# Attention block on one core: the last unit's sums gathered, inverted as 8 columns and spread; partial projections in TensorE's waits; zero products at a higher level

## Chip, cores and metric

One core of one Trainium2 chip. The metric is the device time in microseconds (us) of one execution, the median over runs.

## The reference

Multi-head self-attention with an output projection, in bfloat16, for x of shape (1, 2048, 448), 16 heads of 28:

```python
qkv = (x @ wqkv).reshape(B, S, 3, H, Dh).transpose(2, 0, 3, 1, 4)
q, k, v = qkv[0], qkv[1], qkv[2]
p = softmax(einsum("bhqd,bhkd->bhqk", q, k) * Dh ** -0.5, axis=-1)
o = einsum("bhqk,bhkd->bhqd", p, v)
return o.transpose(0, 2, 1, 3).reshape(B, S, D) @ wo
```

## The kernel before, in words

The work is cut into 16 units: four groups `g` of four heads, and four chunks `c` of 512 queries. In a unit, for each of 16 key tiles `kt` of 128 keys, a "row" is four score tiles of 128 keys by 512 queries, one per head. A score product (L899, TensorE) goes to a PSUM bank; most rows are turned into probabilities by ScalarE's exponential (L961, groups of three and two tiles that alternate between banks 0 to 2 and 3 to 4), into a ring of 43 tile slots `PT`. The 67 rows listed in `PLAN["rows"]` go to VectorE instead, which builds an approximate exponential with integer arithmetic: `DY` (L923, one per head), then two shifted copies `DS` (L931), with three buffers each. The products with V (L866) accumulate a whole unit in one bank of the pool `M` (banks 5 to 7). V has a column of ones, so that row 28 of each head's 32 holds the sum of the softmax.

Behind its last product a unit is normalised. Units 0 to 13 do it through DRAM (L732 to L742). Unit 14 does it on TensorE (`norm_pe`): `N1` (L761) gathers the sums, 4 columns for each 128 queries, by a product of the float copy `OTS` with the selector `SEL`; one reciprocal of 16 columns; `N2` (L772) spreads the inverse over 32 rows per head by products with the identity `id_f`; and a multiply (L776) writes `OTN`. Unit 15, `last_unit` (L781), stands alone at the end. It works in two halves `k` of 256 queries: copy to `OTS` (L803), `BC` (L810), which spreads the sums with the matrix `EX`, a reciprocal of 128x256 into `RB` (L814), the multiply `NM` (L816). Its output projection is split: `OPA` (L792) is three of four groups of heads for each of four output tiles, opened as soon as the score banks (pool `T`) come free, and `OPB` (L833) adds the last group. `out_tile` copies the tile to `OUTS` (ScalarE for even tiles, L699, VectorE for odd, L701) and sends it to DRAM (L703, on ScalarE's queue or SP's). `N1` (L823) and `RS` (L828) then compute the same sums' inverses once more for a range check (L993 to L1005); every engine loads the resulting FLAG at the end (L1689) and branches on it.

The order on each engine is fixed when the program is built, by a list planner (`_Prog.schedule`): every operation has a priority (low goes first), an estimated duration and dependencies; the planner takes on each engine what can start first and, within a look-ahead, what has the lowest priority. `fill_to` puts zero products ("Z", L484, four products of 512 columns that add zero) on TensorE where a gap is long enough or where the activity planned in the last 3413 ns is below a level:

```python
must = 0.0 if -60.0 < nxt.prio < -20.0 or t < self.HOT_UNTIL else CFG["hotm"] if t < CFG["hot1"] else self.FILL_HOT if nxt.kind == "r" and nxt.act > 200.0 else self.FILL_MUST
if level >= self.FILL_TARGET or (level >= must and gap < fd + 15.0):
    return
```

`FILL_HOT` is the level ahead of a score group; `CFG` and `PLAN` hold priorities and the rows and times of the late projections.

Of the kernel before, what the change touches and what calls it, by code (L numbers as in the profile page):

```python
# [7 lines left out]
ALU = mybir.AluOpType  # L8
AX = mybir.AxisListType
FP32 = mybir.dt.float32  # L10
# [53 lines left out]
class _Prog:  # L64
# [276 lines left out]
ZLO = -ZADD  # L341


CFG = {"late": 4.5, "load": 1.5, "load0": 18, "dcost": 2.3, "dlead": 29.327663454, "aslack": 234.39592858, "opp": 0.0, "oload": 2.5, "klead": 0.397755013, "vlag": 0.106640586, "hot1": 45000.0, "hotm": 3600.0, "nslack": 2479.300775199, "dlook": 20.0, "plook": 474.412241514, "rcost": 4.9, "rlead": 1.0, "rend": 4, "rgap": 2, "acost": 0.4455, "dprio": 0.107516791, "nride": 4, "rslack": 300.0, "stail": 24, "jprio": -1.32365559, "sdlap": 1.959518579, "vwlead": 0.625380571, "sdpen": 5.516852626, "rcostx": -0.000676632}

PLAN = {
    "rows": [8, 14, 16, 23, 24, 28, 36, 40, 42, 48, 51, 52, 55, 61, 62, 72, 73, 74, 82, 86, 92, 95, 96, 100, 101, 107, 109, 110, 113, 118, 121, 127, 133, 135, 136, 140, 141, 147, 150, 151, 160, 162, 165, 172, 174, 176, 178, 182, 186, 187, 190, 191, 193, 196, 201, 208, 213, 214, 218, 219, 222, 229, 230, 232, 236, 241, 244],
    "late": [1.077995674, 1.833905636, 2.095141755, 1.212792363, 3.137574495, 1.671785065, 2.075848527, 2.120471152, 2.256950028, 2.271931426, 2.394850262, 3.571309667, 3.864949717, 3.254719197, 2.824659682, 4.377919272, 3.673227809, 4.718144519, 3.955221706, 4.65154477, 4.74737354, 7.012401197, 6.732080085, 7.708659606, 5.168205011, 6.425448937, 5.787055861, 6.854207722, 8.35329498, 10.189712555, 7.674620861, 7.367372235, 8.08547084, 7.336648721, 7.808454674, 8.789731951, 8.769658309, 8.528783968],
}


def _fast(nc, x, wqkv, wo, out, n_heads=16):
# [10 lines left out]
    QCH = 512  # L363
# [18 lines left out]
    units = [(g, c) for g in range(G) for c in range(NCH)]  # L382
# [3 lines left out]
    P = _Prog()  # L386
    es = ExitStack()
    with es:
# [5 lines left out]
        OTN = XO[:, :].rearrange("p (g s) -> p g s", s=S)  # L394
# [60 lines left out]
        def dma_of(t, g):  # L455
# [3 lines left out]
                      dur=300, prio=-12, name="iota")  # L459
# [8 lines left out]
        def zero_pass(acc_open, t):  # L468
# [12 lines left out]
            def emit(e):  # L481
                ins = None
                for h in range(4):
# [15 lines left out]
        ex_op = P.add("dve", (lambda e: e.tensor_copy(EX.rearrange("p (h r) -> p h r", r=32), SEL.rearrange("p (h o) -> p h o", o=1).to_broadcast([128, 4, 32]))),  # L499
                      deps=[sel_op], dur=250, prio=5.0, name="ex")  # L500
        grp_wo = _DmaGroup("wo")
        dma_wo = []
        for g in range(G):
# [117 lines left out]
        rows = PLAN["rows"]  # L621
        if rows is None:
# [5 lines left out]
            rows = []  # L628
# [66 lines left out]
        def out_tile(n, opm, hold, eng, pr):  # L695
            oi = outs_n[0] % NOB
            outs_n[0] += 1
            if eng == "act":
                fe = (lambda e: e.activation(OUTS[:, oi, :], bank(hold.banks[0])[:, 0:D], AF.Identity))  # L699
            else:  # L700
                fe = (lambda e: e.tensor_copy(OUTS[:, oi, :], bank(hold.banks[0])[:, 0:D]))  # L701
            opev = P.add(eng, fe, deps=[opm, outs_last[oi]], dur=550, prio=pr, name=f"OPEV{n}", rel=[(hold, 0)])
            outs_last[oi] = P.add("act" if eng == "act" else "sp", (lambda e: e.dma_start(of[n * 128:(n + 1) * 128, :], OUTS[:, oi, :])),  # L703
                                  deps=[opev], after=[outs_last[oi]], dur=60, prio=pr, name=f"ODMA{n}", dma_group=grp_out[oi],
                                  nbytes=128 * D * 2)
# [75 lines left out]
        def last_unit(u, last_pv):  # L781
            g, c = units[u]
            ub = u % 2
            pr = u - 50.0
            open_ops = []
            for j in range(NQT):
                n = c * NQT + j
                hold = []

                for gg in range(G - 1):  # L790
                    def f_part(e, n=n, hold=hold, gg=gg):
                        return e.matmul(bank(hold[0].banks[0])[:, 0:D], OTN[:, gg, n * 128:(n + 1) * 128], wop[:, gg, :],  # L792
                                        start=(gg == 0), stop=False, skip_group_check=True)
                    op = P.add("pe", f_part, deps=([otn_ev[(g_, c)] for g_ in range(G - 1)] + dma_wo[-1:]) if gg == 0 else [], after=hold[-1:], kind="f", units=0.9, act=448.0,
                               prio=-34.9, name=f"OPA{n}_{gg}", acq=("T", 1) if gg == 0 else None)
                    if gg == 0:
                        hold.append(op)
                open_ops.append((n, hold, op))
            HF = QCH // 2
            evs = []  # L800
            for k in range(2):
                sl = slice(k * HF, (k + 1) * HF)
                evs.append(P.add("dve", (lambda e, sl=sl: e.tensor_copy(OTS[:, ub, sl], bank(pv_open[u].banks[0])[:, sl])),  # L803
                                 deps=[last_pv, ots_last[ub]], after=evs[-1:], dur=340, prio=pr, name=f"ACCEV{u}_{k}", rel=[(pv_open[u], 0)] if k else []))
            bcs, n1s, rss, nms = [], [], [], []
            for k in range(2):
                sl = slice(k * HF, (k + 1) * HF)

                def f_bc(e, k=k, sl=sl):
                    return e.matmul(bank(bcs[k].banks[0])[:, sl], EX, OTS[:, ub, sl], start=True, stop=True)  # L810
                bcs.append(P.add("pe", f_bc, deps=[evs[k], ex_op], after=bcs[-1:], dur=480, prio=pr - 1.0, name=f"BC{u}_{k}", acq=("M", 1)))
            for k in range(2):
                sl = slice(k * HF, (k + 1) * HF)
                rb = P.add("dve", (lambda e, sl=sl, k=k: e.reciprocal(RB[:, ub, sl], bank(bcs[k].banks[0])[:, sl])),  # L814
                           deps=[bcs[k], ots_last[ub]], after=nms[-1:], dur=340, prio=pr - 1.0, name=f"RB{u}_{k}", rel=[(bcs[k], 0)])
                nms.append(P.add("dve", (lambda e, sl=sl: e.tensor_tensor(OTN[:, g, c * QCH + sl.start:c * QCH + sl.stop], RB[:, ub, sl], OTS[:, ub, sl], ALU.mult)),  # L816
                                 deps=[rb, evs[k]], after=nms[-1:], dur=340, prio=pr - 1.0, name=f"NM{u}_{k}"))
            for k in range(2):
                def f_n1(e, k=k):
                    b = n1s[k].banks[0]  # L820
                    ins = None
                    for qt in (2 * k, 2 * k + 1):
                        ins = e.matmul(bank(b)[:, qt * 4:(qt + 1) * 4], OTS[:, ub, qt * 128:(qt + 1) * 128], SEL[:, :], start=True, stop=True)  # L823
                    return ins
                n1s.append(P.add("pe", f_n1, deps=[evs[k], sel_op], after=n1s[-1:] + bcs[-1:], dur=430, prio=-34.85, name=f"N1_{u}_{k}", acq=("M", 1)))
            for k in range(2):
                i0 = u * 16 + 8 * k
                rss.append(P.add("dve", (lambda e, k=k, i0=i0: e.reciprocal(RS[:, i0:i0 + 8], bank(n1s[k].banks[0])[:, 8 * k:8 * k + 8])),  # L828
                                 deps=[n1s[k]], after=rss[-1:] + nms[-1:], dur=120, prio=-34.0, name=f"RS{u}_{k}", rel=[(n1s[k], 0)]))
                rs_last.append(rss[-1])  # L830
            for j, (n, hold, op) in enumerate(open_ops):
                def f_fin(e, n=n, hold=hold):
                    return e.matmul(bank(hold[0].banks[0])[:, 0:D], OTN[:, g, n * 128:(n + 1) * 128], wop[:, g, :], start=False, stop=True, skip_group_check=True)  # L833
                fin = P.add("pe", f_fin, deps=[nms[j // 2]], after=[op], kind="f", units=0.9, act=448.0, prio=pr - 1.0, name=f"OPB{n}")
# [912 lines left out]
```

## Time and profile before

| what | value |
|---|---|
| time, median of 3 runs | 366.27 us (365.79 to 367.6) |
| the profiled execution's own time | 365.65 us |
| its span, first to last instruction | 363.8 us |
| mean granted TensorE clock | 0.997 |
| PE / DVE / ACT busy | 345.0 / 327.5 / 345.7 us |
| exponentials on ScalarE | 303, from 9.77 us to about 353.9 us |

PE is TensorE (PEld its weight loads), DVE VectorE, ACT ScalarE, SP the queue that issues most transfers. In the timeline's rows the numbers are start, duration, engine, line, operation, output<-input, shapes and count; in brackets the idle time before and what ended it. Group rows end with busy time and the mean of one in ns, then the idle time before and what ended it. A row of waits has the total, the times and the longest. A row of a stretch has its length, then busy time and count of PE, PEld, DVE, ACT and POOL, the granted clock, the share of the transfers' engines and GB/s. A matmul's end is modelled, so durations of matmuls that follow each other overlap.

### The profile page before, as it was taken

The page shows a single profiled execution, that of the slowest core. Times are in us where ns is not written, and L with a number is a line of the kernel's source. Part 1 is how long each engine was busy: PE and PEld are TensorE (multiplying, and loading weights), DVE is VectorE, ACT ScalarE, POOL GpSimd, SP SyncE. Part 2 cuts the span into 40 slices and gives each one's busy share as a digit, 9 for nine tenths or more (in the row PEclk, how much of TensorE's full clock was granted, in tenths as well). Part 3 has the DMA queues.
Part 4 walks back from the last instruction along what each step waited for, and adds up shares of the span by engine and source line. Part 5 has one row for each costly group of instructions (what it writes and reads, how often), then busy time and mean ns, then how long its engine had stood idle before and what let it go on. Part 6 is the DMA issues. An engine that isn't in the chain of part 4 may idle for free.

```text
span 363.8 us, 8769 instructions
## 1 busy us (share of the span) xinstructions
PE 345.0 (95%) x3845; PEld 115.1 (32%) x3845; DVE 327.5 (90%) x577; ACT 345.7 (95%) x307; POOL 3.4 (1%) x9
## 2 busy tenths in 40 slices
PE   8999999999999999999999999999998999999995
PEld 4433322333223422233233322332222222223332
DVE  6577999989999999999999999999999999989517
ACT  1999999999999999999999999999999999999991
POOL 3000000000000000000000000000000000000000
PEclk9999999999999999999999999999999999999998
DMA  8500000000000010000100000000000000020201
GB/s 247 134 2 3 3 30 5 19 15 4 30 2 5 32 32 2 3 31 3 28 7 16 20 4 30 3 24 12 30 3 4 30 5 31 4 80 3 77 29 51
DMA packets 13939, 9.89 MB, mean 27 GB/s; under 512 B 7504, under 2 KB 12048, under 8 KB 13896
## 3 DMA queue, kind: packets, MB, share of 16 engines
q1 hardware_dynamic: 13096, 8.74, 8.1%
q8 instruction: 30, 0.49, 0.6%
q10 hardware_dynamic: 800, 0.56, 0.5%
q14 instruction: 13, 0.11, 0.1%
HBM read 7.23 MB, written 2.06 MB: 26 GB/s over the span
## 4 chain that ended last, share of the span: by engine, by line
ACT 80%; PE 17%; DVE 3%; issue 0%
ACT PT L961 80%; PE ps L899 5%; PE ps L866 4%; PE ps L558 2%; PE ps L484 2%; DVE RB L814 1%; PE ps L713 1%; PE ps L575 1%; DVE DY L923 1%; PE ps L541 1%; PE ps L792 0%; DVE DS L931 0%; PE ps L761 0%; PE ps L772 0%; DVE XO L816 0%
## 5 line engine op out<-in xcount | busy, mean ns | idle before, releaser
L961 ACT ACTIVATE PT<-ps 128x1536 bf16<-128x1536 f32 (+1 forms) x303 | 342.7, 1400 | 1.9 <-PE ps L899 1.6
L923 DVE TENSOR_SCALAR DY<-ps 128x512 int16<-128x512 f32 x268 | 175.6, 682 | 10.4 <-PE ps L899 9.2
L899 PE MATMUL ps<-QT,KT 28*128 28x512 bf16 x1024 | 153.1, 384 | 12.2 <-ACT PT L961 6.9
L931 DVE TENSOR_SCALAR DS<-DY 128x2048 int16<-128x2048 int16 x134 | 89.5, 680 | 0.7
L899 PEld LDWEIGHTS ps<-QT,KT 28*128 28x128 bf16 x1024 | 39.8, 91 | 138.5 <-ACT PT L961 101.2
L866 PE MATMUL ps<-PT,V 128*32 128x512 bf16 x756 | 66.5, 385 | 0.9 <-DVE V L531 0.5
L866 PE MATMUL ps<-DS,VW 128*32 128x512 f16 x536 | 48.2, 386 | 0.0
L558 PE MATMUL ps<-xT,w_raw 112*32 112x512 bf16 x512 | 35.8, 381 | 0.1
L484 PE MATMUL ps<-ZM,ZW 128*32 128x512 bf16 x312 | 28.8, 412 | 1.2 <-DVE ZM L466 1.2
L866 PE MATMUL ps<-DY,V 128*32 128x512 f16 x268 | 26.5, 385 | 0.2 <-DVE OTS L726 0.2
L866 PEld LDWEIGHTS ps<-PT,V 128*32 128x32 bf16 x756 | 16.6, 94 | 30.0 <-issue 23.5
L866 PEld LDWEIGHTS ps<-DS,VW 128*32 128x32 bf16 x536 | 12.1, 94 | 21.1 <-issue 16.4
L575 PE MATMUL ps<-w_raw,xT 112*128 112x112 bf16 x256 | 17.3, 214 | 0.0
L558 PEld LDWEIGHTS ps<-xT,w_raw 112*32 112x32 bf16 x512 | 12.5, 95 | 12.9 <-issue 2.9
L701 DVE CAST OUTS<-ps 128x448 bf16<-128x448 f32 x14 | 8.7, 623 | 8.4 <-PE ps L713 8.1
L575 PEld LDWEIGHTS ps<-w_raw,xT 112*128 112x128 bf16 x256 | 13.0, 98 | 6.5 <-issue 4.3
L531 DVE CAST KT<-ps 128x512 bf16<-128x512 f32 x16 | 11.0, 686 | 3.2 <-PE ps L558 3.0
L531 DVE CAST V<-ps 128x448 bf16<-128x448 f32 x16 | 9.9, 618 | 2.6 <-PE ps L575 2.6
L484 PEld LDWEIGHTS ps<-ZM,ZW 128*32 128x32 bf16 x312 | 7.6, 99 | 12.5 <-issue 10.0
L713 PE MATMUL ps<-wop,XO 128*128 128x448 bf16 x48 | 11.5, 355 | 0.0
L529 DVE TENSOR_SCALAR QT<-ps 128x512 bf16<-128x512 f32 x15 | 10.2, 683 | 0.4 <-PE ps L558 0.4
L726 DVE COPY OTS<-ps 128x512 f32<-128x512 f32 x15 | 10.2, 682 | 0.4 <-PE ps L866 0.4
(51 smaller groups left out, 83.8 us busy)
## 6 DMA issues: line engine op xcount, KB each, us to landing
RB<-scr_r SPq DMA_DIRECT2D x14, 256.0 KB
out_dram<-OUTS SPq DMA_DIRECT2D x14, 112.0 KB, 1.7
XO<-in_x_dram SPq DMA_DIRECT2D x3, 448.0 KB, 6.3
w_raw<-in_wqkv_dram SPq DMA_DIRECT2D x5, 196.0 KB, 6.0
wop<-in_wo_dram SPq DMA_DIRECT2D x16, 24.5 KB
XO<-in_x_dram SPq DMA_DIRECT2D x1, 224.0 KB, 3.1
XO<-in_x_dram ACTq DMA_DIRECT2D x1, 224.0 KB, 3.5
scr_l<-OTS SPq DMA_DIRECT2D x14, 8.0 KB
```

The lines of the kernel that those rows point to most:

```text
L484: ins = e.matmul(ps[32 * h:32 * h + 32, b * 512:(b + 1) * 512], ZW[:, :], ZM[:, :], start=shut, stop=shut, skip_group_check=not shut, tile ...
L529: fe = (lambda e: e.tensor_scalar(evac[0](), evac[1](hold[0].banks[0]), mul, None, ALU.mult))
L531: fe = (lambda e: e.tensor_copy(evac[0](), evac[1](hold[0].banks[0])))
L558: ins = e.matmul(ps[32 * h:32 * h + 32, b * 512:(b + 1) * 512], w_raw[0:IT, it, col:col + 32], xT[0:IT, it, c * 512:(c + 1) * 512], start= ...
L575: ins = e.matmul(ps[:, b * 512 + j * GD:b * 512 + (j + 1) * GD], xT[0:IT, it, n * 128:(n + 1) * 128], w_raw[0:IT, it, 2 * D + g * GD:2 * D ...
L713: return e.matmul(bank(hold[0].banks[0])[:, 0:D], OTN[:, gg, n * 128:(n + 1) * 128], wop[:, gg, :], start=(gg == 0), stop=(gg == G - 1))
L726: accev = P.add("dve", (lambda e: e.tensor_copy(OTS[:, ub, :], bank(pv_open[u].banks[0]))), deps=[last_pv, ots_last[ub]], dur=610, prio=pr ...
L866: ins = e.matmul(ps[32 * h:32 * h + 32, b * 512:(b + 1) * 512], weights(k, h), p_[h], start=(kt == 0 and k == 0), stop=(kt == NK - 1 and k ...
L899: ins = e.matmul(bank(b), KT[32 * h:32 * h + rows, g, kt * 128:(kt + 1) * 128], QT[32 * h:32 * h + rows, g, c * QCH:(c + 1) * QCH], start= ...
L923: o1 = P.add("dve", (lambda e, ri=ri, h=h, s=s: e.tensor_scalar(DY[:, ri, h * 512:(h + 1) * 512], bank(s.banks[0]), ZLO, ZADD, ALU.max, AL ...
L931: row_ev[r] = [P.add("dve", (lambda e, k=k: e.tensor_scalar(DS[:, k, rk, :], DY[:, ri, :], float(PHASE[k + 1]), None, ALU.add)), deps=row_ ...
L961: ex = P.add("act", (lambda e, p0=p0, w=w, bf=bf: e.activation(PT[:, p0 * 512:(p0 + w) * 512], bank(bf(), w), AF.Exp, scale=ESCALE)), deps ...
```

## The change

In the last unit `BC`, the two 128x256 reciprocals and `EX` are gone. `N1` and `RS` take their place on the way to `NM`; `N2` spreads the 8 inverted columns of a half over 256 columns, and `NM` reads them from PSUM. Of the twelve `OPA` products the last four are held back to stand in TensorE's order behind `N1`, `N2`, `N2` and the second `OPB`. `FILL_HOT` rises from 2787.5 to 3300. `PLAN` and some priorities in `CFG` are new: again 67 rows on VectorE, others than before, and other times for the 38 late projections.

```diff
-    FILL_HOT = 2787.5
+    FILL_HOT = 3300.0
...
-CFG = {... "dlead": 29.327663454, "aslack": 234.39592858, ... "klead": 0.397755013, "vlag": 0.106640586, ... "nslack": 2479.300775199, ... "dprio": 0.107516791, ... "jprio": -1.32365559, "sdlap": 1.959518579, "vwlead": 0.625380571, "sdpen": 5.516852626 ...}
+CFG = {... "dlead": 30.385592406, "aslack": 235.147215477, ... "klead": 0.405674492, "vlag": 0.024622608, ... "nslack": 2585.717981114, ... "dprio": 0.651412491, ... "jprio": -0.750113813, "sdlap": 4.771128299, "vwlead": 1.249363626, "sdpen": 6.528606395 ...}
...
-    "rows": [... 150, 151, 160, 162, 165, 172, 174, 176, ... 219, 222, 229, 230, 232, 236, 241, 244],
+    "rows": [... 149, 152, 162, 163, 164, 165, 169, 176, ... 215, 222, 229, 231, 234, 235, 244, 248],
...
-        EX = iota_i[:, :].bitcast(FP32)
-        ex_op = P.add("dve", ...)
...
-            bcs, n1s, rss, nms = [], [], [], []
...
-                    return e.matmul(bank(bcs[k].banks[0])[:, sl], EX, OTS[:, ub, sl], start=True, stop=True)
...
-                rb = P.add("dve", (lambda e, sl=sl, k=k: e.reciprocal(RB[:, ub, sl], bank(bcs[k].banks[0])[:, sl])),
-                           deps=[bcs[k], ots_last[ub]], after=nms[-1:], dur=340, prio=pr - 1.0, name=f"RB{u}_{k}", rel=[(bcs[k], 0)])
...
+            n1s, rss, n2s, nms = [], [], [], []
...
-                n1s.append(P.add("pe", f_n1, ..., prio=-34.85, ...))
+                n1s.append(P.add("pe", f_n1, deps=[evs[k], sel_op], after=n1s[-1:], dur=430, prio=pr, name=f"N1_{u}_{k}", acq=("M", 1)))
             for k in range(2):
                 i0 = u * 16 + 8 * k
                 rss.append(P.add("dve", (... e.reciprocal(RS[:, i0:i0 + 8], bank(n1s[k].banks[0])[:, 8 * k:8 * k + 8])),
-                                 deps=[n1s[k]], after=rss[-1:] + nms[-1:], dur=120, prio=-34.0, ...))
+                                 deps=[n1s[k]], after=rss[-1:], dur=200, prio=pr, ...))
+                def f_n2(e, k=k):
+                    for qt in (2 * k, 2 * k + 1):
+                        for h in range(4):
+                            i = u * 16 + qt * 4 + h
+                            ins = e.matmul(ps[32 * h:32 * h + 32, b * 512 + qt * 128:b * 512 + (qt + 1) * 128],
+                                           RS[:, i:i + 1].to_broadcast([128, 32]), id_f[:, :], start=True, stop=True, tile_position=(0, 32 * h))
+                n2s.append(P.add("pe", f_n2, deps=[rss[k]], after=n2s[-1:], dur=400, prio=pr, name=f"N2_{u}_{k}", acq=("M", 1)))
+                nms.append(P.add("dve", (... e.tensor_tensor(OTN[...], bank(n2s[k].banks[0])[:, sl], OTS[:, ub, sl], ALU.mult)),
+                                 deps=[n2s[k]], after=nms[-1:], dur=340, prio=pr, ...))
...
-                fin = P.add("pe", f_fin, ..., prio=pr - 1.0, name=f"OPB{n}")
+                fin = P.add("pe", f_fin, ..., prio=pr if j < 2 else -34.8, name=f"OPB{n}")
+                opb.append(fin)
...
+            for part, behind in ((8, n1s[1]), (9, n2s[1]), (10, n2s[1]), (11, opb[1])):
+                parts_[part].after.append(behind)
+                parts_[part].prio = -36.0
```

More of the change, by code (lines that the diff above doesn't have):

```diff
@@ L349 @@
+    "late": [1.281070854, 1.964014751, 1.915657661, 0.76, 2.743900482, 1.159356603, 1.904466413, 1.845975994, 2.106524837, 2.189415295, 2.428349574, 2.873971098, 2.728623137, 3.84085501, 2.733578841, 4.131340808, 3.508351422, 5.446684044, 4.832243098, 4.46548081, 5.163206443, 7.002171665, 6.90767575, 7.804407036, 4.947925744, 6.78739139, 5.302922841, 6.89552453, 9.777227448, 10.389677342, 7.735503962, 7.490566717, 8.23514301, 7.360578973, 7.83742904, 10.319692841, 8.329224918, 8.680463746],
 }
@@ L784, in last_unit @@
             pr = u - 50.0
-            open_ops = []
+            open_ops, parts_ = [], []
             for j in range(NQT):
@@ L804, in last_unit @@
                                  deps=[last_pv, ots_last[ub]], after=evs[-1:], dur=340, prio=pr, name=f"ACCEV{u}_{k}", rel=[(pv_open[u], 0)] if k else []))
-            bcs, n1s, rss, nms = [], [], [], []
[L806 to L814, printed above, removed]
-                           deps=[bcs[k], ots_last[ub]], after=nms[-1:], dur=340, prio=pr - 1.0, name=f"RB{u}_{k}", rel=[(bcs[k], 0)])
-                nms.append(P.add("dve", (lambda e, sl=sl: e.tensor_tensor(OTN[:, g, c * QCH + sl.start:c * QCH + sl.stop], RB[:, ub, sl], OTS[:, ub, sl], ALU.mult)),
-                                 deps=[rb, evs[k]], after=nms[-1:], dur=340, prio=pr - 1.0, name=f"NM{u}_{k}"))
+            n1s, rss, n2s, nms = [], [], [], []
             for k in range(2):
@@ L828, in last_unit @@
                 rss.append(P.add("dve", (lambda e, k=k, i0=i0: e.reciprocal(RS[:, i0:i0 + 8], bank(n1s[k].banks[0])[:, 8 * k:8 * k + 8])),
-                                 deps=[n1s[k]], after=rss[-1:] + nms[-1:], dur=120, prio=-34.0, name=f"RS{u}_{k}", rel=[(n1s[k], 0)]))
+                                 deps=[n1s[k]], after=rss[-1:], dur=200, prio=pr, name=f"RS{u}_{k}", rel=[(n1s[k], 0)]))
                 rs_last.append(rss[-1])
+                def f_n2(e, k=k):
+                    b = n2s[k].banks[0]
+                    ins = None
+                    for qt in (2 * k, 2 * k + 1):
[3 more added lines that the diff above has]
+                                           RS[:, i:i + 1].to_broadcast([128, 32]), id_f[:, :], start=True, stop=True, tile_position=(0, 32 * h))
+                    return ins
+                n2s.append(P.add("pe", f_n2, deps=[rss[k]], after=n2s[-1:], dur=400, prio=pr, name=f"N2_{u}_{k}", acq=("M", 1)))
+                sl = slice(k * HF, (k + 1) * HF)
+                nms.append(P.add("dve", (lambda e, sl=sl, k=k: e.tensor_tensor(OTN[:, g, c * QCH + sl.start:c * QCH + sl.stop], bank(n2s[k].banks[0])[:, sl], OTS[:, ub, sl], ALU.mult)),
+                                 deps=[n2s[k]], after=nms[-1:], dur=340, prio=pr, name=f"NM{u}_{k}", rel=[(n2s[k], 0)]))
+            opb = []
             for j, (n, hold, op) in enumerate(open_ops):
@@ L833, in f_fin @@
                     return e.matmul(bank(hold[0].banks[0])[:, 0:D], OTN[:, g, n * 128:(n + 1) * 128], wop[:, g, :], start=False, stop=True, skip_group_check=True)
-                fin = P.add("pe", f_fin, deps=[nms[j // 2]], after=[op], kind="f", units=0.9, act=448.0, prio=pr - 1.0, name=f"OPB{n}")
+                fin = P.add("pe", f_fin, deps=[nms[j // 2]], after=[op], kind="f", units=0.9, act=448.0, prio=pr if j < 2 else -34.8, name=f"OPB{n}")
+                opb.append(fin)
                 out_tile(n, fin, hold[0], "act" if j % 2 == 0 else "dve", pr)
+            for part, behind in ((8, n1s[1]), (9, n2s[1]), (10, n2s[1]), (11, opb[1])):
+                parts_[part].after.append(behind)
+                parts_[part].prio = -36.0
         def pv(u, kt):
```

9 lines of the change are left out of this document (3 added, 6 removed).

## The prediction

> **What bounds the kernel now.** I read the page's busy shares first, then the groups, the waits, the chain, and last the timeline of the final 12 us.
>
> ```profile
> PE 345.0 (95%) x3845; PEld 115.1 (32%) x3845; DVE 327.5 (90%) x577; ACT 345.7 (95%) x307; POOL 3.4 (1%) x9
> PEclk9999999999999999999999999999999999999998
> L961 ACT ACTIVATE PT<-ps 128x1536 bf16<-128x1536 f32 (+1 forms) x303 | 342.7, 1400 | 1.9 <-PE ps L899 1.6
> ```
>
> Three engines are 90% busy or more, so the shares alone decide nothing. The group row does: ScalarE's 303 exponentials take 342.7 us of the 363.8 us span and sat idle for 1.9 us before all of them together. ScalarE sets the pace from the first exponential to the last.
>
> ```profile
> PEld ps L899 <- ACT PT L961: 101.2, 271, 0.7
> ACT PT L961 <- PE ps L899: 1.6, 3, 0.6
> 334.50 2.37 ACT L961 ACTIVATE PT<-ps 128x1536 bf16<-128x1536 f32 x2 [0.51 <-PE ps L899]
> 337.45 6.88 ACT L961 ACTIVATE PT<-ps 128x1536 bf16<-128x1536 f32 x6 [0.59 <-PE ps L899]
> ```
>
> These are waits (total, times, longest). TensorE's queue stood 101.2 us, 271 times, until ScalarE gave back a score bank; ScalarE stood 1.6 us for TensorE, in three places. Two of the three lie at 334 and 337 us, 1.1 us together; the third is the start. So the exponentials can lose at most about 1.1 us more of idle time, and the place to gain is behind the last one. The chain there:
>
> ```profile
> 354.31 0.67 PE ps L792 x3
> 354.99 0.57 PE ps L810 x2
> 355.58 1.77 DVE RB L814
> 357.38 0.43 DVE XO L816
> 357.80 1.68 DVE RB L814
> 359.50 0.44 DVE XO L816
> 359.98 0.55 PE ps L833 x2
> 360.54 0.79 PE ps L823 x8
> 361.32 0.89 PE ps L484 x12
> 362.25 0.18 PE ps L1002
> 362.45 0.15 DVE FLAG L1005
> ```
>
> From about 354.3 us on nothing but the last unit's normalisation and projection runs. Two reciprocals of 128x256 elements (RB) take 3.45 us of it. Behind the last projections (359.98) come the reciprocal sums for the flag (L823), zero products (L484), the flag, and the exit.
>
> **The change part by part, first the tail.** Removed: the two spreading products BC, the two RB reciprocals, the start-up copy EX. Moved up from the flag's path onto the main path: the gather N1 (SEL times OTS) and the 8-column reciprocals RS. Added: N2, which spreads the 8 columns with 16 small float products per half, in the form that unit 14 already uses (L772). The rows for the prices:
>
> ```profile
> 354.37 0.76 DVE L803 COPY OTS<-ps 128x256 f32<-128x256 f32 x2 [3.92 <-PE ps L866]
> 354.85 0.73 PEld L810 LDWEIGHTS ps<-OTS,iota_i 128*128 128x128 f32 x4 [0.30 <-DVE OTS L803]
> 332.65 0.83 PE L761 MATMUL ps<-SEL,OTS 128*128 128x4 f32 x6
> 333.74 0.39 PE L761 MATMUL ps<-SEL,OTS 128*128 128x4 f32 x2
> 336.00 1.08 PE L772 MATMUL ps<-id_f,RS 128*32 128x128 f32 x32
> L772 PE MATMUL ps<-id_f,RS 128*32 128x128 f32 x32 | 1.1, 276 | 0.0
> 361.11 0.45 DVE L828 RECIPROCAL RS<-ps 128x8 f32<-128x8 f32 x2
> 359.85 1.35 DVE L701 CAST OUTS<-ps 128x448 bf16<-128x448 f32 x2
> 360.49 0.33 SPq L703 DMA_DIRECT2D out_dram<-OUTS  x1
> 360.49 1.07 SPq L703 DMA_DIRECT2D out_dram<-OUTS  x2
> out_dram<-OUTS SPq DMA_DIRECT2D x3, 112.0 KB, 1.7
> 362.00:362.50 0.50, 0.37 (x5) 0.08 (x1) 0.23 (x2) 0.00 (x0) 0.00 (x0) 0.50 1.04 355
> ```
>
> The copy to OTS still starts at 354.37, and TensorE can take its first half at 354.85 as it does now. N1: six products take 0.83 and two 0.39, so each further one 0.11 and the four of one half 0.61. The first half ends at 354.85 + 0.61 = 355.46, the second, whose loads follow it, 0.45 later at 355.91. RS takes 0.20 to 0.25 each; with 0.04 for the hand-over (in the chain the second NM ends at 359.94 and OPB starts at 359.98) the first ends at 355.70, the second at 356.15. On TensorE the ninth partial projection (0.19: 448 of the 512 columns of a zero pass, which adds 0.21 below) stands between N1 and N2, so N2 starts at 355.85. Thirty-two of its products take 1.08 and one alone 0.276, so sixteen take 0.276 + 15 x 0.026 = 0.67: to 356.52; the second half starts 0.41 behind it and ends at 356.93, its RS being long done. Queued behind the waiting N2 on TensorE are the partials and OPB, behind the waiting NM on VectorE the casts; all of these need NM anyway or have room. N1 and N2 take four banks of pool M's three, but the accumulator's bank is free from 355.13 (354.37 and 0.76) and the first N1's from 355.70.
>
> The multiply NM costs 0.43 as now, reading PSUM instead of RB. The first: 356.56 to 356.99. The two flag comparisons fit into VectorE's wait ahead of it; the minimum CKM (0.17) probably falls between the two multiplies, because the planner starts what is ready first. Behind it wait the second NM and so the last two OPB. I let the second NM run from 357.13 to 357.56. OPB of tiles 0 and 1 run from 357.03; the partials 9 and 10 lie before them in the wait for NM and cost nothing (2 x 0.19 in 356.65 to 357.03, just covered; without that cover up to 0.2). Partial 11 lies after OPB 1. OPB 2 starts at 357.65 where it now starts at 359.98: 2.33 earlier.
>
> The outputs move with it. VectorE's two casts (1.35) can start behind OPB 1 at 357.63 and end at 358.98, against 361.20 now. The last output transfer now issues at about 361.23 (two issues from 360.49 end at 361.56, one is 0.33) and lands 1.7 later, at 362.9. Now it would issue at 359.0 and land at 360.7; ScalarE's third tile issues its own at the same moment, for which I add 0.2: 360.9. (The last stretch quoted moves 355 GB/s, so 112 KB take 0.32; the bounds are zero and that.)
>
> ```profile
> L1689 SPq TENSOR_LOAD <-FLAG x1: 473/473/473, 362.6 to 362.6; - x1
> L1694 SPq EVENT_SEMAPHORE  x2: 17/22/28, 363.2 to 363.3; - x2
> ```
>
> What ends last now is the flag, not the transfer: FLAG ends at 362.60, each queue loads it (0.47), and SP's waits for the outputs stand at 363.2 to 363.3, already satisfied; 0.5 more to 363.8. After the change the flag's chain is ready early, and FLAG stands on VectorE at the latest behind the last cast, at 359.2, so the load ends by 359.7. The transfer is then what is late: 360.9 + 0.5 = 361.4. The tail's gain is 363.8 - 361.4 = **2.4 us**, which I put at 2.35. Bounds: 2.75 if neither CKM nor the shared transfer costs anything, 1.6 if CKM, FLAG ahead of the last cast, a missing cover and 0.32 of sharing all cost.
>
> By the Trainium skill (DMA: Bandwidth & Descriptors, section "Anatomy of one DMA — SWDGE (gpsimd) path") a transfer costs about 2.0 us fixed plus its bytes at 436 GB/s, which is an estimate of 2.26 us for 112 KB and would make the end 0.56 later, a gain of 1.8. The trace's 1.7 decides against it.
>
> EX, one small copy, goes from VectorE's start; it stands beside the loads of x, and I count zero, with its own length as the most that it could give.
>
> **Zero products at a higher level.** FILL_HOT goes from 2787.5 to 3300, about one pass (512) more in a window of 3413 ns.
>
> ```profile
> L484 PE MATMUL ps<-ZM,ZW x248: 379/389/390, 51.8 to 334.8; 128*32 128x512 bf16 x124
> 333.41 0.40 PE L484 MATMUL ps<-ZM,ZW 128*32 128x512 bf16 x4
> 334.59 0.61 PE L484 MATMUL ps<-ZM,ZW 128*32 128x512 bf16 x8
> 354.20:357.80 3.60, 2.15 (x13) 1.08 (x9) 2.94 (x5) 0.00 (x0) 0.00 (x0) 1.00 0.01 2
> 357.80:361.50 3.70, 2.45 (x22) 1.61 (x26) 3.51 (x7) 1.09 (x2) 0.00 (x0) 1.00 0.13 45
> 361.50:363.80 2.30, 0.87 (x13) 0.17 (x5) 0.74 (x5) 0.00 (x0) 0.00 (x0) 0.57 0.38 127
> ```
>
> From 45 us on there are 248 / 4 = 62 passes, 0.21 each (0.61 less 0.40). Weighing the trace's products as the planner does, only about 10 score groups have a level between the two thresholds, so some 10 passes come in, at most one for each of the 62 places: 2.1 to 13 us of TensorE. The cover is the 101.2 us in which TensorE stood for ScalarE; I take zero. Uncovered they would cost 2.1. On the side of a gain there is nothing in this execution: the granted clock (seventh value after the times) is 1.00 in the first two stretches of the tail and 0.57 only at the very end, and the page's row shows nines in all slices before.
>
> **The re-planned rows and projections.** Both plans give 67 rows of scores to VectorE, so 303 exponentials stay. No product or transfer is added; places move. What this does to ScalarE's idle time the trace cannot show. Bounds: 1.1 us gained (both gaps above closed) and, from the zero passes, 2.1 lost; I take zero, since today's plan loses little and the queue that feeds ScalarE has much cover.
>
> **The sum.** 2.35 off the profiled execution's 365.65 us (span 363.8 and 1.85 around it) is 363.3. That execution lies 0.6 under the median 366.27, so against the median: **363.9**.
>
> **The rivals.**
> *Middle gives it back* (0.20). The new order puts zero passes or late projections ahead of score groups that have no cover; seven or so uncovered passes (7 x 0.21 = 1.5) give 365.4. For it: ScalarE lost 1.1 us at 334 to 337, beside zero passes. Against it: the 101.2 us.
> *Middle improves* (0.12). The gaps of 0.51 and 0.59 go, as the rows after 222 stand otherwise: 362.9.
> *Slower through VectorE* (0.06). The new plan has rows 162 to 165 all on VectorE; today at most three stand together, 72 to 74.
>
> ```profile
> L923 DVE TENSOR_SCALAR DY<-ps 128x512 int16<-128x512 f32 x268 | 175.6, 682 | 10.4 <-PE ps L899 9.2
> L931 DVE TENSOR_SCALAR DS<-DY 128x2048 int16<-128x2048 int16 x134 | 89.5, 680 | 0.7
> ```
>
> A row costs 4 x 0.655 + 2 x 0.668 = 3.96 us of VectorE, four 15.8. With three row buffers the fourth row waits for the first one's product. ScalarE runs on into 43 slots of 342.7/756 = 0.453 us each, 19.5 us. It stalls only when row 165 is later than that; it decides for "slower" when it is 2.35 + 1.83 = 4.2 us beyond, at 23.7. Then about 369.
> *The tail is mis-sized* (0.10). Half of that is the clock: with TensorE at half clock between the last score product and the last projection, the chain's 0.61 + 0.67 + 0.62 of products would grow by some 1.0, gain 1.35, time 364.9. Today TensorE is busy for 2.15 of 3.60 and 2.45 of 3.70 us in the tail and the clock holds 1.00 to 361.5; the new tail stands no more. The Trainium skill (TensorE: Matmul & The Clock Gate, "Part 1: The HAM clock gate") has the gate halve the clock after an idle window of about 3.4 us; the trace agrees, as the two stretches have at most 1.45 and 1.25 us of gap. The other half is a zero pass or the flag's product put ahead of N2 or OPB, or the flag still last: about 365.
>
> **How the numbers follow.** The forecast has 0.52, with a range of its own of 363.3 to 364.4. Half a per cent is 1.83 us, about what a measurement of this kernel tells from no change: 364.44 and 368.1. Faster: forecast and improved middle, 0.64. Same: the given-back middle and the mis-sized tail, 0.29. Slower: VectorE's case and 0.01 of the given-back middle, 0.07. The range runs from 2.75 + 1.1 under the median, 362.4, to the upper part of the given-back middle, 366.0.
>
> **What would show it.** In the profile after: no 128x256 reciprocal; 8-column ones ahead of NM; from the last product with V to the first OPB about 3.1 us and to the third about 3.7 instead of 6.0; a last output transfer that ends behind the flag. ScalarE's exponentials again near 342.7 us with 1 to 2 us of idle. About 72 zero passes after 45 us. Wrong would be: ScalarE's waits for scores above 3 us, score groups in VectorE's wake, a granted clock under 1.00 before the last transfer, or the flag's load still last.

## The result and the profile after

The changed kernel takes 362.34 us (median of 5 runs, 362.02 to 363.91), the kernel before, measured beside it, 366.21 us (5 runs, 365.65 to 367.60). The ratio is 0.9898, with a 95% interval of 0.9868 to 0.9929: 1% faster. The forecast was 363.9; the result lies 0.06 us below the low end of its range, 362.4; as a ratio that end is 0.9894 (362.4 / 366.27), and the measured 0.9898 lies within. The profiled execution took 362.26 us, its span 360.4 (before 365.65 and 363.8).

The page of the changed kernel, with the rows that answer those of before (group rows end with busy time, mean ns of one, and idle time before):

```profile
span 360.4 us, 8848 instructions
PE 342.2 (95%) x3885; PEld 114.4 (32%) x3885; DVE 321.8 (89%) x574; ACT 345.5 (96%) x307; POOL 3.4 (1%) x9
PEclk9999999999999999999999999999999999999999
L966 ACT ACTIVATE PT<-ps 128x1536 bf16<-128x1536 f32 (+1 forms) x303 | 342.5, 1398 | 1.0 <-PE ps L904 0.9
```

And its row of ScalarE's waits for scores (total, times, longest):

```profile
ACT PT L966 <- PE ps L904: 0.9, 2, 0.5
```

ScalarE still has its 303 exponentials, but waited 0.9 us for scores where it waited 1.6, twice instead of three times. So the saving is not only in the tail. I cut each span at the first exponential, the end of the last one and the start of the last product with V:

| us | before | after | difference |
|---|---|---|---|
| start, to the first exponential | 9.774 | 9.422 | -0.352 |
| first exponential to the end of the last | 344.089 | 343.030 | -1.059 |
| to the start of the last product with V | 0.062 | 0.063 | 0 |
| tail, from there to the end | 9.843 | 7.866 | -1.977 |
| span | 363.77 | 360.38 | -3.39 |

The middle's 1.06 us is 0.84 less idle time of ScalarE (gaps of 0.148, 0.126, 0.505 and 0.586 before, 0.067 and 0.457 after) and 0.22 less time in the exponentials themselves.

The tail in the timeline of the changed kernel (start, duration, engine, line; in brackets the idle time before and what ended it; the last product with V starts at 352.51):

```profile
352.96 0.76 DVE L801 COPY OTS<-ps 128x256 f32<-128x256 f32 x2 [6.38 <-PE ps L871]
353.44 1.05 PE L809 MATMUL ps<-SEL,OTS 128*128 128x4 f32 x8
354.08 0.21 DVE L814 RECIPROCAL RS<-ps 128x8 f32<-128x8 f32 x1 [0.37 <-PE ps L809]
354.35 0.35 PE L789 MATMUL ps<-wop,XO 128*128 128x448 bf16 x1
354.63 0.81 PEld L824 LDWEIGHTS ps<-id_f,RS 128*32 128x32 f32 x32 [0.21 <-issue]
354.63 1.08 PE L824 MATMUL ps<-id_f,RS 128*32 128x128 f32 x32
355.34 0.43 DVE L829 TENSOR_TENSOR XO<-ps,OTS 128x256 bf16<-128x256 f32 x1 [0.18 <-PE ps L824]
355.64 0.11 PEld L789 LDWEIGHTS ps<-wop,XO 128*128 128x128 bf16 x2 [0.20 <-issue]
355.64 0.55 PE L789 MATMUL ps<-wop,XO 128*128 128x448 bf16 x2
356.03 0.54 PE L834 MATMUL ps<-wop,XO 128*128 128x448 bf16 x2
356.42 0.54 ACT L696 ACTIVATE OUTS<-ps 128x448 bf16<-128x448 f32 x1 [3.97 <-PE ps L834]
356.60 0.54 PE L834 MATMUL ps<-wop,XO 128*128 128x448 bf16 x2
356.61 1.19 DVE L698 CAST OUTS<-ps 128x448 bf16<-128x448 f32 x2 [0.41 <-PE ps L834]
357.00 0.38 ACTq L700 DMA_DIRECT2D out_dram<-OUTS  x1
357.47 0.54 ACT L696 ACTIVATE OUTS<-ps 128x448 bf16<-128x448 f32 x1 [0.51 <-PE ps L1007]
357.72 0.13 DVE L1010 TENSOR_SCALAR FLAG<-ps 1x1 int32<-1x1 f32 x1
358.05 0.35 ACTq L700 DMA_DIRECT2D out_dram<-OUTS  x1
```

Where two reciprocals of 1.68 to 1.77 us stood, two of 0.21 do, and the four OPB (L834) run at 356.03 and 356.60. The flag is ready at 357.85. What ends last is the output that ScalarE issues at 358.05: by the trace's landing times it arrives at 359.84, SP's last one at 359.53, and the program ends 0.54 later.

The other place is unit 14's normalisation. The same stretch of the two timelines, first before, then after:

```profile
334.34 1.22 DVE L931 TENSOR_SCALAR DS<-DY 128x2048 int16<-128x2048 int16 x2
335.13 0.49 PEld L713 LDWEIGHTS ps<-wop,XO 128*128 128x128 bf16 x4 [0.42 <-DVE DS L931]
335.99 0.81 PEld L772 LDWEIGHTS ps<-id_f,RS 128*32 128x32 f32 x32 [0.37 <-DVE CK L993]
337.01 0.60 PE L899 MATMUL ps<-QT,KT 28*128 28x512 bf16 x5
```

```profile
331.19 0.25 DVE L760 RECIPROCAL RS<-ps 128x16 f32<-128x16 f32 x1
331.70 0.83 PE L484 MATMUL ps<-ZM,ZW 128*32 128x512 bf16 x12
332.36 1.05 PE L769 MATMUL ps<-id_f,RS 128*32 128x128 f32 x32
333.34 0.60 PE L904 MATMUL ps<-QT,KT 28*128 28x512 bf16 x5
333.78 5.97 ACT L966 ACTIVATE PT<-ps 128x1536 bf16<-128x1536 f32 x5 [0.46 <-PE ps L904]
```

Before, the normalisation cut the scores twice: the gather and a zero pass (shown with the prediction) ahead of those at 334.06, which cost the gap of 0.51, then two zero passes, four products of the output projection (L713) and the spreading product ahead of those at 337.01, which cost 0.59. From 334.59 to 337.01 TensorE is busy without a break; the 0.42 and 0.37 that the rows put down to VectorE are waits of the weight loads alone, behind products that still run. After, the gather at 329.17 costs ScalarE nothing, the projections stand elsewhere, and three zero passes with the spreading product leave one gap of 0.46. Which of the new rows and times moved the projections away was not tested.

### The profile page after: what moved, and what is told of

Same layout as the page of the kernel before. It is cut to its first block, busy times and chain, and to the rows that moved or that the text cites. A ratio compares the mean times of both kernels' runs of the same rounds, so it can differ in the third digit from the quotient of the medians.

```text
span 360.4 us, 8848 instructions
## 1 busy us (share of the span) xinstructions
PE 342.2 (95%) x3885; PEld 114.4 (32%) x3885; DVE 321.8 (89%) x574; ACT 345.5 (96%) x307; POOL 3.4 (1%) x9
## 4 chain that ended last, share of the span: by engine, by line
ACT 88%; PE 11%; issue 0%; ACTq 0%; DVE 0%
ACT PT L966 87%; PE ps L904 3%; PE ps L871 2%; PE ps L555 2%; PE ps L484 1%; PE ps L789 1%; PE ps L572 0%; PE ps L538 0%; ACT OUTS L696 0%; PE ps L824 0%; PE ps L758 0%; PE ps L809 0%; PE ps L769 0%; PE ps L710 0%; ACT QT L524 0%
## 5 line engine op out<-in xcount | busy, mean ns | idle before, releaser
L871 PE MATMUL ps<-DS,VW 128*32 128x512 f16 x536 | 49.3, 385 | 0.1
```

Source lines behind the costliest of these rows:

```text
L871: ins = e.matmul(ps[32 * h:32 * h + 32, b * 512:(b + 1) * 512], weights(k, h), p_[h], start=(kt == 0 and k == 0), stop=(kt == NK - 1 and k ...
```

## The experiments

**Which part gave what: the last unit alone, the plan alone.** `e1_tail` is the kernel before with the changed `last_unit` and without `EX`; `e2_plan` is the kernel before with the new `FILL_HOT`, `CFG` and `PLAN` and the old last unit.

> The kernel before with the changed last unit alone (and without EX); FILL_HOT, CFG and PLAN are the old ones, so TensorE's order is the old one up to the last unit. Theory A (the tail and the plan add up): from the start of the last product with V to the end of the span about 7.9 us instead of 9.84, so 2.0 us off; ScalarE's idle time between exponentials stays near 1.4 us with the gaps of about 0.5 and 0.6 at 334 to 337; time about 2.0 us (0.55%) under before. Rival B (the plan carries most of it): the shorter tail is given back by the exit or by late partials, at most 1.0 us under before.

> The kernel before with the new FILL_HOT, CFG and PLAN and the old last unit (BC, two 128x256 reciprocals, EX). Theory A: the tail stays at 9.8 us; ScalarE's idle time between exponentials falls from 1.37 to about 0.5 us with one gap of 0.45 near 334; time 0.8 to 1.1 us under before (0.2 to 0.3%). Rival B: 2 us or more under before. Rival C (EX's copy at the start delays the first exponential by 0.35 us): first exponential at 9.77 us, as EX is there.

| | time, us | ratio to before | exponentials, first to last | tail |
|---|---|---|---|---|
| before (same call) | 367.25 | | 344.09 | 9.84 |
| e1_tail | 363.99 | 0.9912 [0.9880, 0.9945] | 344.09 | 7.87 |
| e2_plan | 364.55 | 0.9933 [0.9907, 0.9959] | 343.03 | 11.27 |
| after | 362.34 | 0.9898 [0.9868, 0.9929] | 343.03 | 7.87 |

(The last two columns are from one profiled execution each; the ratio in the last row is to the 366.21 us measured beside it.) In the profiles the two parts separate and add: the last unit alone leaves the middle as it was, with the same gaps, and has the whole gain of the tail; the plan alone has the whole gain of the middle. The medians don't add (3.26 and 2.70 us under 367.25, and 3.87 for both under 366.21), as the executions of the kernel before spread over 3 us. The lowest times nearly do: 365.68 falls to 363.22 and to 364.33, by 2.46 and 1.35, and for both 365.65 to 362.02, by 3.63.

The tail of `e2_plan` is the old one, and yet 1.43 us longer than in the kernel before. Its stretches show where (length, busy time and count of PE, PEld, DVE, ACT, POOL, then the granted clock):

```profile
356.00:358.00 2.00, 0.93 (x4) 0.31 (x4) 1.97 (x3) 0.54 (x1) 0.00 (x0) 1.00 0.00 0
358.00:360.00 2.00, 1.23 (x6) 0.97 (x6) 1.48 (x4) 0.54 (x1) 0.00 (x0) 0.50 0.17 57
360.00:362.00 2.00, 2.00 (x18) 1.41 (x18) 1.23 (x6) 0.00 (x0) 0.00 (x0) 0.50 0.51 172
```

While TensorE waited for the long reciprocals its clock fell to half at 358.0, ahead of the last projections, in this profiled execution. That is the clock rival's mechanism, met in the old tail. The clock rose at 6.43 us, and 358.0 is 103 times 3.413 us later. In the last such 3.41 us, from 354.59 on, TensorE was busy for 1.48 us. In the kernel before they end at 358.41, hold 1.91 us of work, and the clock stays, though its longest wait in the tail is the same, 1.50 us. So it seems to matter how these stretches lie to the tail; how much work is enough was not measured. In the profile after the clock holds 1.00 to the last instruction of TensorE:

```profile
354.00:356.00 2.00, 2.00 (x40) 1.45 (x40) 1.43 (x7) 0.00 (x0) 0.00 (x0) 1.00 0.04 8
356.00:358.00 2.00, 1.24 (x8) 0.47 (x5) 1.45 (x4) 1.07 (x2) 0.00 (x0) 1.00 0.05 16
```

**Do the held-back partials pay?** `e4_no_hold` is the changed kernel without the loop that holds them; the planner then puts all four behind the first two OPB.

```diff
-            for part, behind in ((8, n1s[1]), (9, n2s[1]), (10, n2s[1]), (11, opb[1])):
-                parts_[part].after.append(behind)
-                parts_[part].prio = -36.0
```

> The changed kernel without the rule that holds back the last four partial projections; the planner then puts two of them behind N2 ahead of the first OPB, and two... behind the first pair of OPB, as its priorities have it; all else is the same order. If the held partials are covered (as the prediction counted, ahead of the first OPB), the tail of 7.87 us grows by up to 0.2. If they are not covered anywhere (0.19 us each on TensorE's path), nothing changes within 0.1 us but where they stand: four of them still cost about 0.4 to 0.8 us of the tail.

362.03 us, ratio 0.9863 [0.9828, 0.9897]. The tail is 7.71 us, 0.16 shorter than with the loop, in one profile each. Its timeline, where the last product with V starts at 352.27:

```profile
354.18 1.08 PE L824 MATMUL ps<-id_f,RS 128*32 128x128 f32 x32
355.37 0.55 PE L834 MATMUL ps<-wop,XO 128*128 128x448 bf16 x2
356.51 0.54 PE L834 MATMUL ps<-wop,XO 128*128 128x448 bf16 x2
```

N2 starts 1.91 us behind that product and the first OPB 3.10; with the loop it is 2.12 and 3.52. The third comes later than with the loop, 4.24 for 4.09, and yet the program ends earlier: the transfer of tile 12 is issued at 356.34, before tile 14 is ready, and ScalarE's copy of tile 14 no longer waits for it. So by these profiles the loop costs where it holds up the first OPB; in the times, 362.03 and 362.34, the two don't separate.

**Was the start copy worth something?** `e7_ex` puts `EX` back into the changed kernel, with no reader.

> The changed kernel with EX's copy put back at VectorE's start, with no reader; nothing else moves on TensorE. Rival C (EX delays the first exponential): it starts at about 9.77 us instead of 9.42 and the whole kernel is 0.35 us longer. Theory A (the 0.35 us is TensorE's clock at the start: in the profile before, the first transposes are 107 ns apart to 6.4 us, in the one after only to 5.4 us and 56 ns from there): the first exponential falls anywhere from 9.2 to 9.8 us, whether or not EX is there, and the time stays within 0.4 us of the changed kernel's 362.3.

362.49 us, 0.9873 [0.9837, 0.9909]; middle and tail as after (343.03 and 7.86). The first exponential stands at 9.86, 0.44 later than after. But over all kernels this does not go with `EX`: with it 9.17 to 9.90, without it 9.17 to 9.83. What it goes with is below, under the hardware.

**Do zero products alone steady the old tail?** `e10_old_zero` is the kernel before with eleven small zero passes, six between the two spreading products and the first OPB and five between the second and third, to keep TensorE active there.

> The kernel before with eleven zero products of four in the old tail: six in TensorE's wait for the first 128x256 reciprocal, five in the wait for the second; they add zero to open output tiles. Theory D (TensorE's clock falls to half in the old tail in part of the executions, because it stands idle there; one of the profiles, e2_plan, has it at 0.50 from 358.0 us on and a tail of 11.3 us instead of 9.8): the slow executions near 368 us go away, all lie within 365.4 to 366.8, the median falls by about 1 us under the kernel before in the same call, and the tail in the profile stays at 9.8 us. Rival (the two groups of times have another cause): as many executions near 368 us as in the kernel before.

365.89 us (12 runs, 365.23 to 368.59), 0.9993 [0.9972, 1.0015]: no difference. The tail took 10.02 us, 0.18 longer than in the kernel before, with the clock full. Two of the twelve runs were still above 367. The mean granted clock of each execution is on record: 8 of the 12 have 0.999 or 1.000, which none of the 17 of the kernel before in this call has (0.998 at most), and the other four, with 0.991 to 0.995, are the four longest, 366.58 to 368.59. So the long executions are those with the lower clock, which speaks against the rival; the added products keep it up in part of the executions, and the time is not clear of no change.

**Is the higher level free by itself?** `e6_fill_high` is the kernel before with `FILL_HOT = 3300.0` and nothing else.

> The kernel before with FILL_HOT at 3300 alone (old CFG, PLAN and last unit). The prediction: about ten zero passes more and nothing in the time. Theory A now: with the old plan the passes are re-ordered from 20 us on; exponentials idle between 1.2 and 2.5 us instead of 1.37, tail 9.8 us, time within 1 us of before. (With the new plan the level changes no instruction at all: planned with 2787.5 the program is the same, so it has no share in the gain.) Rival (the level is what gains): 1 us or more under before.

374.99 us, 1.0228 [1.0189, 1.0267]: 8.7 us slower. Two rows of its page, then one of its waits:

```profile
L484 PE MATMUL ps<-ZM,ZW 128*32 128x512 bf16 x404 | 36.6, 415 | 1.2 <-DVE ZM L466 1.2
L961 ACT ACTIVATE PT<-ps 128x1536 bf16<-128x1536 f32 (+1 forms) x303 | 343.4, 1347 | 6.9 <-PE ps L866 3.7
```

```profile
ACT PT L961 <- PE ps L899: 3.0, 6, 1.6
```

Zero products rise from 312 to 404, 23 passes, and the exponentials' idle time from 1.9 to 6.9 us; first to last exponential takes 349.85 us, and the last product with V comes 3.0 us behind the last exponential instead of 0.06. On the old plan the level is dear.

**And the lists without each other?** `e13_cfg` is the changed kernel with the old `PLAN`, `e15_rows` the changed kernel with the old `CFG`, both with the new level and last unit.

> The changed kernel with the old PLAN (rows and times of the late projections) and the new CFG and FILL_HOT. If the lists carry the 1.06 us of the middle, they are gone here: 344 us or more from first to last exponential. If CFG carries them, 343.0. If lists and CFG only fit together, clearly more than 344.1.

> The changed kernel with the new PLAN and the old CFG (FILL_HOT 3300). Same question from the other side: 343.0 us from first to last exponential if the lists carry the gain, 344 if CFG does, clearly more than 344.1 if only both together do.

372.53 us, 1.0168 [1.0121, 1.0215], and 369.97 us, 1.0094 [1.0062, 1.0125]. With the new tail in both, they are slower than before: each loses several times what the plan gains as a whole. The waits of `e13_cfg`, then of `e15_rows`:

```profile
ACT PT L966 <- PE ps L904: 4.8, 6, 1.9
ACT PT L966 <- PE ps L871: 3.3, 2, 1.7
```

```profile
ACT PT L966 <- PE ps L871: 3.9, 2, 3.6
ACT PT L966 <- PE ps L904: 2.6, 4, 1.0
```

Only the new costs and rows together give the quiet middle. With both of them the level decides nothing: planned at 2787.5 the changed kernel has the same instructions in the same order on every engine.

**Passes or order?** To see whether the 23 added passes or the order around them cost `e6_fill_high` its time, `e11_high_noz` is that kernel with the zero passes planned between 45 and 340 us not issued, and `e12_before_noz` the kernel before with the same edit.

> e6_fill_high's order on every engine (old plan, FILL_HOT 3300: 375.0 us, 8.7 over before), but the zero products that the planner placed between 45 and 340 us are not issued. If the added passes themselves hold the score groups up, ScalarE's idle time falls from 5.4 us towards 1.5 and the time towards 367 to 369. If the other order is what costs (the planner, moving one pass, sets everything behind it differently), idle time and the late last products with V stay and the time stays at 372 or more. If the granted clock falls without the passes, the middle grows instead.

> The kernel before with its 62 zero passes between 45 and 340 us not issued, all else in the same order. If they are covered and the clock does not need them: 343.1 to 344.1 us from the first to the last exponential (344.09 now), the gaps at 334 to 337 shorter by up to 0.6 us. If the clock needs them, it falls to 0.50 for at least one stretch of 3.4 us in the units with little other work (250 to 310 us), and the time grows by 1 us or more.

406.11 us (two runs, 402.89 and 409.34) and 389.74 us (384.57 and 394.92). Both are far slower, so the question they were to answer is not answered. What they show is what the passes are for. Of `e12_before_noz` the clock row and the exponentials, then two of its stretches:

```profile
PEclk9999999999999999778999758997865599699998
L961 ACT ACTIVATE PT<-ps 128x1536 bf16<-128x1536 f32 (+1 forms) x303 | 345.3, 1348 | 17.2 <-PE ps L899 16.4
```

```profile
140.00:190.00 50.00, 46.09 (x472) 13.79 (x468) 44.25 (x77) 46.63 (x42) 0.00 (x0) 0.86 0.04 13
...
290.00:340.00 50.00, 46.56 (x375) 11.15 (x371) 44.12 (x76) 46.09 (x41) 0.00 (x0) 0.79 0.07 20
```

Without 62 passes (13 us of TensorE at 0.21 each) the clock is granted at 0.79 to 0.86 over the stretches from 140 to 340 us, TensorE becomes late and ScalarE stands 17 us.

**What the passes at unit 14 cost, and the best version.** `e8_noz` is the changed kernel with no zero passes next to unit 14's N2. `e9_best` adds to it that only one partial stands ahead of the first OPB, behind N2, and that tile 12's output goes out on SP's queue.

```diff
-            while self.FILL is not None:
+            while self.FILL is not None and not nxt.name.startswith("N2_14") and not (order["pe"] and order["pe"][-1].name.startswith("N2_14")):
...
-            for part, behind in ((8, n1s[1]), (9, n2s[1]), (10, n2s[1]), (11, opb[1])):
+            for part, behind in ((8, n2s[1]), (9, opb[1]), (10, opb[1]), (11, opb[1])):
...
-                P.add("act" if eng == "act" else "sp", ...)
+                P.add("act" if eng == "act" and n % 4 else "sp", ...)
```

> The changed kernel without zero products right before and right behind unit 14's N2 (331 to 333 us). In the changed kernel three passes (0.63 us) stand there between the reciprocal's end at 331.4 and N2, and ScalarE then idles 0.46 us at 333.8. If these passes are what is uncovered, the gap closes and first to last exponential falls from 343.03 to about 342.6 us, time 0.4 us under the changed kernel. If N2 and the projections cost it, the gap stays at 0.4 us or more.

> Meant to beat both: e8_noz, and in the last unit only the ninth partial projection ahead of the first OPB, the other three behind the second, and the first tile's transfer to DRAM on SP's queue, so that ScalarE copies tiles 0 and 2 one after the other. From e4_no_hold's trace: first OPB 3.1 us behind the last product with V, third and fourth at 4.0 to 4.2, VectorE's last cast ends at 5.1 instead of 5.3, its transfer is last. Tail 7.5 us instead of 7.87; with the gap closed the span is 0.8 us under the changed kernel's at the same clock at the start, time about 361.5.

`e8_noz`: 362.22 us, 0.9879 [0.9850, 0.9908]. Its gap there is 0.216 instead of 0.457, first to last exponential 342.79:

```profile
335.29 4.63 ACT L966 ACTIVATE PT<-ps 128x1024 bf16<-128x1024 f32 x4 [0.22 <-PE ps L904]
```

About half of the gap was the passes, by one profile each; in the time, 362.22 for 362.34, it does not show. `e9_best`: 361.74 us (361.51 to 361.97), 0.9866 [0.9837, 0.9895]; tail 7.55. Rows of its timeline, with the last product with V at 352.64:

```profile
355.76 0.54 PE L834 MATMUL ps<-wop,XO 128*128 128x448 bf16 x2
357.09 0.54 ACT L696 ACTIVATE OUTS<-ps 128x448 bf16<-128x448 f32 x1 [0.40 <-PE ps L834]
357.67 0.38 ACTq L700 DMA_DIRECT2D out_dram<-OUTS  x1
```

The first OPB is 3.12 us behind the product and ScalarE's last output issues 5.03 behind it instead of 5.53. From the first exponential to the end `e9_best` takes 350.40 us, the changed kernel 350.96. The intervals of the times overlap; the 0.56 is from one profile each.

## Why the prediction was right and where it was wrong

**Right: the mechanism of the tail.** The wide reciprocals were the price, and of their replacement these pieces cost what their rows said (first half of N1 ends 1.54 us behind the last V product, as worked out; the reciprocals 0.21 each; sixteen products of N2 0.65 for 0.67; the multiply 0.43), and the flag is no longer last.

**Mis-sized: the tail's gain, 1.98 for 2.35, a term 0.37 too large, inside its bounds of 1.6 to 2.75.** Two steps failed. First, "the partials 9 and 10 ... cost nothing ... just covered": they start 0.20 behind N2's last weight load (`<-issue`) and still run when the multiply ends, so the first OPB comes 0.26 behind it (355.77 to 356.03) where 0.04 was forecast. N2 itself starts 0.19 later than worked out, 2.12 behind the V product for 1.93, because the gather was priced too low: its eight weight loads take 0.97 us, and in `e4_no_hold`, with no partial between, N2 follows right behind them at 1.91, where the working without the partial's 0.19 gives 1.74. So the first OPB comes at 3.52 instead of 3.1, the third at 4.09 instead of 3.7. Second, the step that took SP's transfer for the last: ScalarE's queue is later, because tile 14's copy waits for tile 12's transfer to be issued (357.00 to 357.41). Tile 14 is issued 5.53 us behind the V product where 5.1 was forecast, and lands in 1.79 where 1.9 was. Had SP's last transfer (359.53) ended the program, the tail would have been 7.56, so this step is worth 0.31 of the 0.37; `e9_best`, which takes the cause away, has 7.55. VectorE's casts were better than forecast (1.19 for 1.35) and made up part of the first step.

**The clock's half of *the tail is mis-sized*** did not come in the profile after. But its argument, that waits as short as today's leave the clock full, does not hold for the old tail: `e2_plan` has the same longest wait of TensorE, 1.50 us, and its clock halved.

**Wrong: "I take zero" for the middle.** It gained 1.06 us, close to the bound of 1.1, which left out two small gaps (0.148 and 0.126); 0.22 of the gain is shorter exponentials, a term that the working does not have and whose cause stays open. This is the rival *middle improves*, held at 0.12, on top of the tail. The rival itself named the place, unit 14's two gaps; the trace could not show whether the new rows free it. The argument for zero, that today's plan loses little, is true and does not exclude losing less.

**Right in outcome, wrong as an argument: the higher level at zero cost.** There are 70 passes after 45 us (280 products) where 72 were forecast, and they cost about 0.24 us at one place, the passes at unit 14's N2. But the level has no share in them: with the new costs and rows it changes nothing. On the old order, on which "some 10 passes" were reckoned, it brings 23, and 5.8 us more from the first exponential to the last. The 101.2 us in which TensorE stood for ScalarE did not cover that; whether the passes themselves cost it or the other order around them stays open. *Middle gives it back* was the true risk of that edit alone.

**Not weighed: the start**, 0.35 us, and not the change's doing (below). **EX at zero** holds. **VectorE's rows 162 to 165** brought no gap.

So the profiled execution came out at 362.26 for the 363.3 forecast: -0.35 start, -1.06 middle, +0.37 tail. The remaining 0.5 of the 1.56 between forecast and median comes from the step that set the new median 0.6 above its profiled execution, as it stood before; it stands 0.08 above. The old tail can lose 1.4 us to the clock, as `e2_plan` shows, and the record of each execution's mean granted clock fits this as the cause: of 36 executions of the kernel before beside the experiments, the 11 with 0.997 or more took 365.57 to 366.45 us, the 8 with 0.988 or less 367.77 to 368.56, and the 17 between 366.10 to 368.71. The changed kernel has 0.999 or 1.000 in four of its five, and 0.995 in the one that took 363.91. Where in an execution the clock fell is known of the profiled ones alone.

## What to carry to other kernels

When every step of a serial tail has a row of its own kind, its sum can be trusted to a few tenths; look there for the weight loads of short products, and for issue time on the queue that sends the last output. Idle time of the pacing engine beside a known event, here 1.1 us at unit 14, is a gain that a reordering may take: price it, don't set it to zero because it is small. Settings of a planner (level, costs, rows) are one thing: against the kernel before, the level alone cost 2.3%, and the level with the costs alone or the rows alone 1.7 and 0.9%, in spite of the new tail.

## What the hardware showed

TensorE's clock starts at half and first rises between 4.1 and 7.1 us into the span, and the start follows it. The transposes of x, first before, then after:

```profile
4.75 1.96 PE L541 MATMUL ps<-id_b,XO 128*112 128x128 bf16 x16
9.77 1.45 ACT L961 ACTIVATE PT<-ps 128x1536 bf16<-128x1536 f32 x1 [0.49 <-PE ps L899]
```

```profile
4.79 1.59 PE L538 MATMUL ps<-id_b,XO 128*112 128x128 bf16 x16
9.42 1.45 ACT L966 ACTIVATE PT<-ps 128x1536 bf16<-128x1536 f32 x1 [0.49 <-PE ps L904]
```

They follow each other by 107 ns until the clock's record rises and by 56 ns after it: at 6.84 us before, at 5.50 after, so that half of them were already short. Where it rose at 4.75 to 4.78 (`e10_old_zero`, `e4_no_hold`) the first exponential came at 9.17, where it rose at 6.87 to 7.09 (`e7_ex`, `e8_noz`, `e9_best`, `e12_before_noz`) at 9.79 to 9.90. `e1_tail` is an exception, 4.08 and 9.43, and `e15_rows` another, 5.42 and 9.60. Where the clock stays full up to the tail, the lengths of full clock in the records are 351.57, 354.99, 358.40 and 361.81 us, 103 to 106 times 3.413. The Trainium skill (TensorE: Matmul & The Clock Gate, "Part 1: The HAM clock gate") says that the activity window is 3413 ns, runs free of the kernel's start, and so moves the transition by some 500 ns; the multiples agree with it, but the transition moved by 3.0 us here, and the measurement decides.

Second, a row's "issue" need not be a price of its own. The rows put 0.21 us of it between a partial projection (128x128 weights) and N2's products (128x32), and 0.20 behind N2. Without a partial between N1 and N2, `e4_no_hold` and `e9_best` start N2 1.91 us behind the last V product instead of 2.12: the partial costs 0.21 in all, and 0.19 was counted for its columns alone. A separate price of the switch between the two forms is not shown.
